# Loading and rotating the first batch under the table generation, and moving two weight casts from VectorE to ScalarE

## The chip, the cores and the metric

One core of a Trainium2 chip. The metric is the time of one execution on the device in microseconds (us), the median of several executions. "Span" is the profiler's length of one execution, from its first to its last instruction; it lies about 2 us under the time. The granted clock is the share of its full clock that TensorE gets; where it is 0.50 TensorE is called cold, at 1.00 warm. All runs told of here are in the fast state, with a mean granted clock of 0.97 to 1.00.

## The reference

A spectral mixing layer, then a two-layer network with an ELU between its layers, over 8 batches of 3008 x 256:

```python
X = np.fft.rfft(x, axis=1)                  # x: (8, 3008, 256) -> 1505 frequencies
Yr = Xr @ w_r - Xi @ w_i + b_r              # complex channel mixing, 256 x 256
Yi = Xr @ w_i + Xi @ w_r + b_i
Y  = soft_threshold(Yr, 0.01) + 1j * soft_threshold(Yi, 0.01)
y  = np.fft.irfft(Y, n=3008, axis=1)
h  = y.reshape(24064, 256) @ w_in           # 256 -> 2048
g  = np.where(h > 0, h, np.exp(np.minimum(h, 0)) - 1)
return g @ w_out                            # 2048 -> 256
```

## The kernel before

Both Fourier transforms are matmuls against tables of cosines and sines (`CT`, `ST`: 1505 x 1505, bf16), which the kernel generates itself, once, at its start. The real input is first folded: rows u(a) and v(S-a) give `ur` = u + v and `ui` = u - v ("the rotation": TensorE reverses the rows with a permutation matrix into `rps`, in PSUM, the memory space in which the kernel places the results of its matmuls; VectorE adds and subtracts). Then `fps` is the forward transform, `mps` the channel mixing, `psP`/`psQ` the inverse transform, `hps` and `ps_o` the network.

The set-up, with cuts marked:

```python
with tc.tile_pool(name="stagep", bufs=1) as stagep, tc.tile_pool(name="genp", bufs=2) as genp:
    # ... DMA of w_r, w_i, biases, then w_in_f and w_out_f (2 MB each), on SyncE's queue
    # ... four small casts of w_r, w_i to wcat_r, wcat_s
    nc.vector.tensor_scalar_mul(w_in_s_bf[:], w_in_f[:], s_scale)
    nc.vector.tensor_copy(w_out_r[:], w_out_f[:])
    # ... permutation matrices, index rows (brow, acol)
    for (g0, g1) in CH:                      # columns 0-512, 512-1024, 1024-1505
        for t in range(NT):                  # 12 tiles of 128 rows
            # ScalarE prod = brow*acol; VectorE qz (three operations); ScalarE ST = Sin(qz)
            # VectorE absw = |qz|;      ScalarE CT = Sin(pi/2 - absw)
    # ... two row scalings of CT by 0.5; column sum cs_ps of w_out_f and the bias rows bb_ps on TensorE

wk1 = ctx.enter_context(tc.tile_pool(name="wk1", bufs=1))
for b in range(B):
    Ut = wk1.tile([P, NT, D], F32R, name="Ut", tag="Ut")
    Vs = wk1.tile([P, NT, D], F32R, name="Vs", tag="Vs")
    # ... four nc.gpsimd.dma_start of batch b into Ut and Vs
    # ... rotation: rps -> ur, ui
    for kc, (k0, k1) in enumerate(CH):       # forward transform
        for comp, usrc, msrc, xdst in ((0, ur, CT, XrT), (1, ui, ST, XsT)):
            for dt in range(2):
                # 12 matmuls into fps, then nc.vector.tensor_copy(xdst[...], fps[...])
    # ... mps, psP, psQ, hps, ps_o, output
```

`wk1` is opened after the set-up pools are closed, so `Ut` and `Vs` lie where the set-up's tiles lay.

## Time and profile before

Median 1530.85 us (4 runs, 1530.05 to 1531.21), span 1528.7 us, mean granted clock 0.973. The prediction below reads the pieces of the set-up from the trace; they follow one another, weights, tables, load of batch 0, rotation and forward transform, and what comes behind them, 1389.3 us, is TensorE bound. The number to follow is the start of the first channel-mixing matmul (`mps`), called the milestone: 139.43. Columns of the order of time in the prediction: start us, us, engine, line, operation, out<-in, shapes, count, and in brackets the idle time before and what ended it.

```profile
3.96 0.42 DVE L93 TENSOR_SCALAR wcat_s<-w_r_f 128x512 bf16<-128x512 f32 x1
16.83 9.63 PE L166 MATMUL cs_ps<-w_out_f,ones_f 128*128 128x256 f32 x32 [16.83 <-DMA w_out_f<-in_moe_w_out_dram]
```

The small weight cast takes 0.42 us with nothing beside it, and the column sum runs at 16.83, under the tables, where it costs nothing.

### The profile page before, as it was taken

Reading aid. Unit: us, or ns where it says so; the run is one execution under the profiler, and the core shown is the slowest. Engines: PE = TensorE matmul, PEld = TensorE weight load, DVE = VectorE, ACT = ScalarE, POOL = GpSimd, SP = SyncE. Lnnn points to the kernel's source line nnn. Section 1 sums busy time; section 2 is a strip of 40 time slices with the busy share of each in tenths; the row PEclk is TensorE's granted clock in tenths of the full one; section 3 lists DMA queues with packets and bytes.
Section 4 is the critical chain, followed back from the end, with each engine's and each line's share of the span. In section 5 each row is a group of like instructions: output and inputs, shape, how many; then the busy total and the mean of one; then the engine's idle time right before and its main releaser. Section 6 shows DMA issues by size and latency. Waiting matters only on the chain.

```text
span 1528.7 us, 20423 instructions
## 1 busy us (share of the span) xinstructions
PE 1379.3 (90%) x7434; PEld 802.4 (52%) x7434; DVE 998.7 (65%) x1888; ACT 874.7 (57%) x1697; POOL 30.6 (2%) x45
## 2 busy tenths in 40 slices
PE   2039999989999899989999899999999899998998
PEld 2013466535664366635665356644665356643555
DVE  7945486565764587664875677654875657745666
ACT  6920199605992089703994069901996059920897
POOL 1010000000000000000000000000000000000000
PEclk8559999999999999999999999999999999999999
DMA  3061040000410040100400013000400000100001
GB/s 124 0 128 36 0 110 28 27 1 1 116 36 13 0 96 29 40 1 0 110 29 26 1 42 83 28 13 1 110 29 26 1 0 29 42 12 0 15 28 40
DMA packets 52905, 55.58 MB, mean 36 GB/s; under 512 B 1594, under 2 KB 52548, under 8 KB 52548
## 3 DMA queue, kind: packets, MB, share of 16 engines
q0 software_dynamic: 24960, 24.91, 7.6%
q1 hardware_dynamic: 27844, 29.37, 5.5%
q8 instruction: 58, 0.95, 0.3%
q14 instruction: 43, 0.35, 0.1%
HBM read 29.63 MB, written 24.64 MB: 36 GB/s over the span
## 4 chain that ended last, share of the span: by engine, by line
PE 80%; DVE 15%; issue 2%; DMA 1%; ACT 1%; POOL 0%; SPq 0%; DVEq 0%; ACTq 0%; POOLq 0%
PE ps_o L375 26%; PE fps L248 16%; PE hps L351 11%; PE hps L358 10%; PE psP L298 8%; PE psQ L310 8%; DVE yb L280 4%; DVE Yit L286 2%; DVE Yrt L283 2%; DVE gT L370 1%; DVE qz L148 1%; DVE absw L153 1%; DVE osb L385 1%; DVE qz L142 1%; DVE qz L145 1%
## 5 line engine op out<-in xcount | busy, mean ns | idle before, releaser
L370 DVE SCALAR_TENSOR_TENSOR gT<-Et,Rt 128x512 fp32r<-128x512 f32 (+1 forms) x768 | 518.6, 680 | 190.9 <-ACT Rt L369 140.1
L375 PE MATMUL ps_o<-w_out_r,gT 128*128 128x256 f32 (+1 forms) x3072 | 597.7, 317 | 7.9 <-DVE gT L370 6.2
L375 PEld LDWEIGHTS ps_o<-w_out_r,gT 128*128 128x128 f32 (+1 forms) x3072 | 428.8, 186 | 197.0 <-DVE gT L370 160.8
L366 ACT ACTIVATE Et<-hps 128x512 f32<-128x512 f32 (+1 forms) x768 | 455.2, 593 | 71.4 <-DVE gT L370 25.7
L369 ACT ACTIVATE Rt<-hps 128x512 bf16<-128x512 f32 (+1 forms) x768 | 452.5, 589 | 0.0
L306 ACT CAST Psb<-psP 128x512 bf16<-128x512 f32 (+1 forms) x48 | 27.8, 579 | 558.1 <-PE psP L298 558.1
L351 PE MATMUL hps<-yT,w_in_s_bf 128*128 128x512 bf16 (+1 forms) x768 | 294.8, 384 | 1.8 <-ACT Rt L369 1.7
L358 PE MATMUL hps<-yT,w_in_s_bf 128*128 128x512 bf16 (+1 forms) x768 | 288.3, 375 | 0.0
L248 PE MATMUL fps<-CTmat,ur 128*128 128x512 bf16 (+1 forms) x576 | 153.5, 379 | 0.5 <-DVE ui L232 0.5
L317 DVE TENSOR_TENSOR yT<-Psb,psQ 128x512 bf16<-128x512 bf16 (+1 forms) x48 | 32.6, 679 | 169.5 <-PE psQ L310 169.5
L248 PE MATMUL fps<-STmat,ui 128*128 128x512 bf16 (+1 forms) x576 | 140.3, 376 | 0.0
L298 PE MATMUL psP<-CTmat,Yrt 128*128 128x512 bf16 (+1 forms) x576 | 131.4, 375 | 4.7 <-DVE yb L280 4.7
L310 PE MATMUL psQ<-STmat,Yit 128*128 128x512 bf16 (+1 forms) x576 | 131.4, 375 | 0.0
L351 PEld LDWEIGHTS <-w_in_s_bf 128*128 128x128 bf16 x768 | 73.7, 96 | 44.5
L298 PEld LDWEIGHTS <-Yrt 128*128 128x128 bf16 x576 | 56.0, 97 | 74.3 <-issue 6.9
L310 PEld LDWEIGHTS <-Yit 128*128 128x128 bf16 x576 | 56.0, 97 | 65.4
L248 PEld LDWEIGHTS <-ur 128*128 128x128 bf16 x576 | 56.5, 98 | 64.1 <-issue 2.8
L248 PEld LDWEIGHTS <-ui 128*128 128x128 bf16 x576 | 53.9, 97 | 61.6 <-issue 1.0
L358 PEld LDWEIGHTS <-w_in_s_bf 128*128 128x128 bf16 x768 | 76.2, 99 | 14.2 <-issue 3.1
L255 DVE CAST XrT<-fps 128x512 bf16<-128x512 f32 (+1 forms) x48 | 32.7, 682 | 67.5 <-PE fps L248 67.5
L255 DVE CAST XsT<-fps 128x512 bf16<-128x512 f32 (+1 forms) x48 | 32.8, 683 | 66.0 <-PE fps L248 66.0
L385 DVE TENSOR_TENSOR osb<-ps_o,colsum_bc 128x256 f32<-128x256 f32 x192 | 67.8, 416 | 7.7 <-PE ps_o L375 7.0
(70 smaller groups left out, 759.0 us busy)
## 6 DMA issues: line engine op xcount, KB each, us to landing
out_dram<-osb SPq DMA_DIRECT2D x40, 512.0 KB, 2.8
Ut<-in_x_dram POOLq DMA_DIRECT2D x8, 1408.0 KB, 7.8
Vs<-in_x_dram POOLq DMA_DIRECT2D x8, 1408.0 KB, 9.3
out_dram<-osb SPq DMA_DIRECT2D x8, 384.0 KB, 2.5
w_in_f<-in_moe_w_in_dram SPq DMA_DIRECT2D x1, 2048.0 KB, 8.4
w_out_f<-in_moe_w_out_dram SPq DMA_DIRECT2D x1, 2048.0 KB, 13.8
Vs<-in_x_dram POOLq DMA_DIRECT2D x8, 128.0 KB, 2.9
Ut<-in_x_dram POOLq DMA_DIRECT2D x8, 97.0 KB, 6.9
```

Source lines behind the costliest of these rows:

```text
L248: nc.tensor.matmul(fps[:, 0:kw], lhsT=usrc[0:npt, t, dt * P : dt * P + P], rhs=msrc[0:npt, t, k0:k1], start=(t == 0), stop=(t == NT - 1),)
L255: nc.vector.tensor_copy(xdst[:, dt, k0:k1], fps[:, 0:kw])
L280: nc.vector.tensor_tensor(yb[0:kn], psk, bias_bc[0:kn, :], ALU.add)
L298: nc.tensor.matmul(psP[:, 0:nw], lhsT=Yrt[0:npt, t, dt * P : dt * P + P], rhs=CT[0:npt, t, n0:n1], start=(t == 0), stop=(t == NT - 1),)
L310: nc.tensor.matmul(psQ[:, 0:nw], lhsT=Yit[0:npt, t, dt * P : dt * P + P], rhs=ST[0:npt, t, n0:n1], start=(t == 0), stop=(t == NT - 1),)
L351: nc.tensor.matmul(hps[:, 0:nb], lhsT=w_in_s_bf[:, 0, ft * P : ft * P + P], rhs=yT[:, 0, bs:be], start=True, stop=False,)
L358: nc.tensor.matmul(hps[:, 0:nb], lhsT=w_in_s_bf[:, 1, ft * P : ft * P + P], rhs=yT[:, 1, bs:be], start=False, stop=True,)
L366: nc.scalar.activation(Et[:, 0:nb], hps[:, 0:nb], AF.Exp)
L369: nc.scalar.activation(Rt[:, 0:nb], hps[:, 0:nb], AF.Relu)
L370: nc.vector.scalar_tensor_tensor(gT[:, 0:nb], Et[:, 0:nb], 1.0, Rt[:, 0:nb], ALU.min, ALU.add)
L375: nc.tensor.matmul(ps_o[i][0:tn, :], lhsT=gT[:, t0:t1], rhs=w_out_r[:, ft, :], start=(ft == 0), stop=(ft == NFT - 1),)
L385: nc.vector.tensor_tensor(osb[0:tn, i, :], ps_o[i][0:tn, :], colsum_bc[0:tn, :], ALU.subtract)
```

## The change

Intent: give `Ut`, `Vs`, `ur` and `ui` memory of their own from the start, so that the first batch can be loaded and rotated while the tables are generated and its forward transform can follow them chunk by chunk; and take the two big weight casts out of VectorE's way. Core of the diff, cuts marked by `# ...`:

```diff
+    wk1a = ctx.enter_context(tc.tile_pool(name="wk1a", bufs=1))   # Ut, Vs, ur, ui, XrT, XsT
+    def emit_load(b):              # the four DMAs, body as before
+    def emit_rot(Ut, Vs):          # the rotation, body as before
+    def emit_main(b, ur, ui, pools):   # forward transform and all after it, as before
     with (stagep, genp):
-        w_r_f = stagep.tile([P, 2, D], F32, name="w_r_f")
+        w_st = wk1a.tile([P, NT // 2, D], F32, name="w_st", tag="ui")   # staging in ui's memory
         # ...
-        nc.vector.tensor_scalar_mul(w_in_s_bf[:], w_in_f[:], s_scale)
-        nc.vector.tensor_copy(w_out_r[:], w_out_f[:])
         # ... index rows now ahead of the permutation matrices
+        UV0 = emit_load(0)
         for (g0, g1) in CH:
             for t in range(NT):
                 # ... as before, but tabs[g0, t] = the absw operation, last_act = the cosine
-        nc.vector.tensor_scalar_mul(CT[0:1, 0, :], CT[0:1, 0, :], 0.5)      # and one more, over all columns
+            nc.vector.tensor_scalar_mul(CT[0:1, 0, g0:g1], ..., 0.5)        # and one more, per chunk
+            if g0 == 0:
+                with tc.issue_after(tabs[0, 10].ins):
+                    ur0, ui0 = emit_rot(*UV0)
+        with tc.issue_after(last_act.ins):
+            nc.scalar.activation(w_in_s_bf[:], w_in_f[:], AF.Copy, bias=0.0, scale=s_scale)
+            nc.scalar.copy(w_out_r[:], w_out_f[:])
         # ... column sum and bias rows as before
+    # ... wk1b (Yrt, Yit, yT), wk2, wk3
+    for b in range(B):
+        if b == 0:
+            ur, ui = ur0, ui0
+        else:
+            ur, ui = emit_rot(*emit_load(b))
+        emit_main(b, ur, ui, pools)
```

`issue_after` places what stands under it behind the named instruction in its engine's order.

More of the change, by code (lines that the diff above doesn't have):

```diff
@@ L71 @@
     psO = ctx.enter_context(tc.tile_pool(name="psO", bufs=4, space=bass.MemoryType.PSUM))
-    with (
-        tc.tile_pool(name="stagep", bufs=1) as stagep,
-        tc.tile_pool(name="genp", bufs=2) as genp,
-    ):
-        w_r_f = stagep.tile([P, 2, D], F32, name="w_r_f")
-        nc.sync.dma_start(w_r_f[:], w_r.rearrange("(c p) e -> p c e", p=P))
-        w_i_f = stagep.tile([P, 2, D], F32, name="w_i_f")
-        nc.sync.dma_start(w_i_f[:], w_i.rearrange("(c p) e -> p c e", p=P))
-        b_r_row = stagep.tile([1, D], F32, name="b_r_row")
-        b_i_row = stagep.tile([1, D], F32, name="b_i_row")
-        nc.sync.dma_start(b_r_row[:], b_r.rearrange("(o d) -> o d", o=1))
-        nc.sync.dma_start(b_i_row[:], b_i.rearrange("(o d) -> o d", o=1))
-        w_in_f = stagep.tile([P, 2, DFF], F32, name="w_in_f")
-        nc.sync.dma_start(w_in_f[:], moe_w_in.rearrange("(c p) f -> p c f", p=P))
-        w_out_f = stagep.tile([P, NFT, E], F32, name="w_out_f")
-        nc.sync.dma_start(w_out_f[:], moe_w_out.rearrange("(t p) e -> p t e", p=P))
-        nc.vector.tensor_copy(wcat_r[:, :, 0:D], w_r_f[:])
-        nc.vector.tensor_copy(wcat_r[:, :, D : 2 * D], w_i_f[:])
-        nc.vector.tensor_copy(wcat_s[:, :, 0:D], w_i_f[:])
-        nc.vector.tensor_scalar_mul(wcat_s[:, :, D : 2 * D], w_r_f[:], -1.0)
-        nc.vector.tensor_scalar_mul(w_in_s_bf[:], w_in_f[:], s_scale)
-        nc.vector.tensor_copy(w_out_r[:], w_out_f[:])
-        nc.gpsimd.memset(ones_f[:], 1.0)
-        jtmp = genp.tile([P, P], F32, name="jtmp", tag="jt")
-        nc.gpsimd.memset(jtmp[:], 0.0)
-        nc.gpsimd.affine_select(
-            out=jtmp[:], in_=jtmp[:], pattern=[[1, P]], compare_op=ALU.not_equal,
-            fill=1.0, base=-(P - 1), channel_multiplier=1,
-        )
-        nc.vector.tensor_copy(J_mid[:], jtmp[:])
-        jtmp2 = genp.tile([P, P], F32, name="jtmp2", tag="jt")
-        nc.gpsimd.memset(jtmp2[:], 0.0)
-        nc.gpsimd.affine_select(
-            out=jtmp2[:], in_=jtmp2[:], pattern=[[1, P]], compare_op=ALU.not_equal,
-            fill=1.0, base=-P, channel_multiplier=1,
-        )
-        nc.vector.tensor_copy(J_first[:], jtmp2[:])
-        jtmp3 = genp.tile([P, P], F32, name="jtmp3", tag="jt")
-        nc.gpsimd.memset(jtmp3[:], 0.0)
-        nc.gpsimd.affine_select(
-            out=jtmp3[:], in_=jtmp3[:], pattern=[[1, P]], compare_op=ALU.not_equal,
-            fill=1.0, base=0, channel_multiplier=1,
-        )
-        nc.vector.tensor_copy(E00[:], jtmp3[:])
-        brow_i = genp.tile([P, F], I32, name="brow_i", tag="gi")
-        nc.gpsimd.iota(brow_i[:], pattern=[[1, F]], base=0, channel_multiplier=0)
-        acol_i = genp.tile([P, NT], I32, name="acol_i", tag="gi2")
-        nc.gpsimd.iota(acol_i[:], pattern=[[P, NT]], base=0, channel_multiplier=1)
-        brow = genp.tile([P, F], F32, name="brow", tag="g0")
-        nc.vector.tensor_copy(brow[:], brow_i[:])
-        acol = genp.tile([P, NT], F32, name="acol", tag="g3")
-        nc.vector.tensor_copy(acol[:], acol_i[:])
-        sin_scale = 2.0 * math.pi / S * (1.0 - 3e-7)
-        invS = 1.0 / S
-        CMAGIC = 12582912.0
-        cbias = genp.tile([P, 1], F32, name="cbias", tag="cb")
-        nc.vector.memset(cbias[:], math.pi / 2.0)
-        for (g0, g1) in CH:
-            gw = g1 - g0
-            for t in range(NT):
-                prod = genp.tile([P, 512], F32, name="prod", tag="g1")
-                nc.scalar.activation(
-                    prod[:, 0:gw], brow[:, g0:g1], AF.Copy, bias=0.0, scale=acol[:, t : t + 1]
-                )
-                qz = genp.tile([P, 512], F32, name="qz", tag="g2")
-                nc.vector.tensor_scalar(
-                    qz[:, 0:gw], prod[:, 0:gw], invS, CMAGIC, ALU.mult, ALU.add
-                )
-                nc.vector.tensor_scalar(
-                    qz[:, 0:gw], qz[:, 0:gw], -CMAGIC, -float(S), ALU.add, ALU.mult
-                )
-                nc.vector.tensor_tensor(qz[:, 0:gw], qz[:, 0:gw], prod[:, 0:gw], ALU.add)
-                nc.scalar.activation(
-                    ST[:, t, g0:g1], qz[:, 0:gw], AF.Sin, bias=0.0, scale=sin_scale
-                )
-                absw = genp.tile([P, 512], F32, name="absw", tag="g3b")
-                nc.vector.scalar_tensor_tensor(
-                    absw[:, 0:gw], qz[:, 0:gw], -1.0, qz[:, 0:gw], ALU.mult, ALU.max
-                )
-                nc.scalar.activation(
-                    CT[:, t, g0:g1], absw[:, 0:gw], AF.Sin, bias=cbias[:], scale=-sin_scale
-                )
-        nc.vector.tensor_scalar_mul(CT[0:1, 0, :], CT[0:1, 0, :], 0.5)
-        nc.vector.tensor_scalar_mul(
-            CT[LASTP - 1 : LASTP, NT - 1, :], CT[LASTP - 1 : LASTP, NT - 1, :], 0.5
-        )
-        cs_ps = psAcc.tile([P, 512], F32, name="cs_ps", tag="acc")
-        for ft in range(NFT):
-            nc.tensor.matmul(
-                cs_ps[:, 0:E],
-                lhsT=ones_f[:, 0:P],
-                rhs=w_out_f[:, ft, :],
-                start=(ft == 0),
-                stop=(ft == NFT - 1),
-            )
-        nc.scalar.copy(colsum_bc[:], cs_ps[:, 0:E])
-        bcatF = stagep.tile([1, 2 * D], F32, name="bcatF")
-        nc.vector.tensor_copy(bcatF[:, 0:D], b_r_row[:])
-        nc.vector.tensor_copy(bcatF[:, D : 2 * D], b_i_row[:])
-        bb_ps = psAcc.tile([P, 512], F32, name="bb_ps", tag="acc")
-        nc.tensor.matmul(bb_ps[:, 0 : 2 * D], lhsT=ones_f[0:1, 0:P], rhs=bcatF[:, :], start=True, stop=True)
-        nc.scalar.copy(bias_bc[:], bb_ps[:, 0 : 2 * D])
@@ L182 @@
-    wk1 = ctx.enter_context(tc.tile_pool(name="wk1", bufs=1))
-    wk2 = ctx.enter_context(tc.tile_pool(name="wk2", bufs=2))
-    wk3 = ctx.enter_context(tc.tile_pool(name="wk3", bufs=3))
+    wk1a = ctx.enter_context(tc.tile_pool(name="wk1a", bufs=1))
     out2d = out
-    for b in range(B):
+    def emit_load(b):
         xb = x[b]
-        Ut = wk1.tile([P, NT, D], F32R, name="Ut", tag="Ut")
-        Vs = wk1.tile([P, NT, D], F32R, name="Vs", tag="Vs")
+        Ut = wk1a.tile([P, NT, D], F32R, name="Ut", tag="Ut")
+        Vs = wk1a.tile([P, NT, D], F32R, name="Vs", tag="Vs")
@@ L204 @@
         )
-        ur = wk1.tile([P, NT, D], BF16, name="ur", tag="ur")
-        ui = wk1.tile([P, NT, D], BF16, name="ui", tag="ui")
+        return Ut, Vs
+    def emit_rot(Ut, Vs):
+        ur = wk1a.tile([P, NT, D], BF16, name="ur", tag="ur")
+        ui = wk1a.tile([P, NT, D], BF16, name="ui", tag="ui")
         for j in range(NT // 2):
@@ L234 @@
                 )
-        XrT = wk1.tile([P, 2, F], BF16, name="XrT", tag="XrT")
-        XsT = wk1.tile([P, 2, F], BF16, name="XsT", tag="XsT")
+        return ur, ui
+    def emit_main(b, ur, ui, pools):
+        wk1b, wk2, wk3 = pools
+        XrT = wk1a.tile([P, 2, F], BF16, name="XrT", tag="XrT")
+        XsT = wk1a.tile([P, 2, F], BF16, name="XsT", tag="XsT")
         for kc, (k0, k1) in enumerate(CH):
@@ L255 @@
                     nc.vector.tensor_copy(xdst[:, dt, k0:k1], fps[:, 0:kw])
-        Yrt = wk1.tile([P, NT, D], BF16, name="Yrt", tag="Yrt")
-        Yit = wk1.tile([P, NT, D], BF16, name="Yit", tag="Yit")
+        Yrt = wk1b.tile([P, NT, D], BF16, name="Yrt", tag="Yrt")
+        Yit = wk1b.tile([P, NT, D], BF16, name="Yit", tag="Yit")
         for kt in range(NT):
@@ L289 @@
             )
-        yT = wk1.tile([P, 2, S], BF16, name="yT", tag="yT")
+        yT = wk1b.tile([P, 2, S], BF16, name="yT", tag="yT")
         for dt in range(2):
@@ L399 @@
                 )
+    with (
+        tc.tile_pool(name="stagep", bufs=1) as stagep,
+        tc.tile_pool(name="genp", bufs=2) as genp,
+    ):
+        w_st = wk1a.tile([P, NT // 2, D], F32, name="w_st", tag="ui")
+        w_r_f = w_st[:, 0:2, :]
+        nc.sync.dma_start(w_r_f, w_r.rearrange("(c p) e -> p c e", p=P))
+        w_i_f = w_st[:, 2:4, :]
+        nc.sync.dma_start(w_i_f, w_i.rearrange("(c p) e -> p c e", p=P))
+        b_r_row = stagep.tile([1, D], F32, name="b_r_row")
+        b_i_row = stagep.tile([1, D], F32, name="b_i_row")
+        nc.sync.dma_start(b_r_row[:], b_r.rearrange("(o d) -> o d", o=1))
+        nc.sync.dma_start(b_i_row[:], b_i.rearrange("(o d) -> o d", o=1))
+        w_in_f = stagep.tile([P, 2, DFF], F32, name="w_in_f")
+        nc.sync.dma_start(w_in_f[:], moe_w_in.rearrange("(c p) f -> p c f", p=P))
+        w_out_f = stagep.tile([P, NFT, E], F32, name="w_out_f")
+        nc.sync.dma_start(w_out_f[:], moe_w_out.rearrange("(t p) e -> p t e", p=P))
+        nc.vector.tensor_copy(wcat_r[:, :, 0:D], w_r_f)
+        nc.vector.tensor_copy(wcat_r[:, :, D : 2 * D], w_i_f)
+        nc.vector.tensor_copy(wcat_s[:, :, 0:D], w_i_f)
+        nc.vector.tensor_scalar_mul(wcat_s[:, :, D : 2 * D], w_r_f, -1.0)
+        brow_i = wk1a.tile([P, NT * D // 2], I32, name="brow_i", tag="ur")
+        nc.gpsimd.iota(brow_i[:, 0:F], pattern=[[1, F]], base=0, channel_multiplier=0)
+        acol_i = stagep.tile([P, NT], I32, name="acol_i")
+        nc.gpsimd.iota(acol_i[:], pattern=[[P, NT]], base=0, channel_multiplier=1)
+        brow = stagep.tile([P, F], F32, name="brow")
+        nc.vector.tensor_copy(brow[:], brow_i[:, 0:F])
+        acol = stagep.tile([P, NT], F32, name="acol")
+        nc.vector.tensor_copy(acol[:], acol_i[:])
+        nc.gpsimd.memset(ones_f[:], 1.0)
+        jtmp = stagep.tile([P, P], F32, name="jtmp")
+        nc.gpsimd.memset(jtmp[:], 0.0)
+        nc.gpsimd.affine_select(
+            out=jtmp[:], in_=jtmp[:], pattern=[[1, P]], compare_op=ALU.not_equal,
+            fill=1.0, base=-(P - 1), channel_multiplier=1,
+        )
+        nc.vector.tensor_copy(J_mid[:], jtmp[:])
+        jtmp2 = stagep.tile([P, P], F32, name="jtmp2")
+        nc.gpsimd.memset(jtmp2[:], 0.0)
+        nc.gpsimd.affine_select(
+            out=jtmp2[:], in_=jtmp2[:], pattern=[[1, P]], compare_op=ALU.not_equal,
+            fill=1.0, base=-P, channel_multiplier=1,
+        )
+        nc.vector.tensor_copy(J_first[:], jtmp2[:])
+        jtmp3 = stagep.tile([P, P], F32, name="jtmp3")
+        nc.gpsimd.memset(jtmp3[:], 0.0)
+        nc.gpsimd.affine_select(
+            out=jtmp3[:], in_=jtmp3[:], pattern=[[1, P]], compare_op=ALU.not_equal,
+            fill=1.0, base=0, channel_multiplier=1,
+        )
+        nc.vector.tensor_copy(E00[:], jtmp3[:])
+        UV0 = emit_load(0)
+        tabs = {}
+        sin_scale = 2.0 * math.pi / S * (1.0 - 3e-7)
+        invS = 1.0 / S
+        CMAGIC = 12582912.0
+        cbias = stagep.tile([P, 1], F32, name="cbias")
+        nc.vector.memset(cbias[:], math.pi / 2.0)
+        for (g0, g1) in CH:
+            gw = g1 - g0
+            for t in range(NT):
+                prod = genp.tile([P, 512], F32, name="prod", tag="g1")
+                nc.scalar.activation(
+                    prod[:, 0:gw], brow[:, g0:g1], AF.Copy, bias=0.0, scale=acol[:, t : t + 1]
+                )
+                qz = genp.tile([P, 512], F32, name="qz", tag="g2")
+                nc.vector.tensor_scalar(
+                    qz[:, 0:gw], prod[:, 0:gw], invS, CMAGIC, ALU.mult, ALU.add
+                )
+                nc.vector.tensor_scalar(
+                    qz[:, 0:gw], qz[:, 0:gw], -CMAGIC, -float(S), ALU.add, ALU.mult
+                )
+                nc.vector.tensor_tensor(qz[:, 0:gw], qz[:, 0:gw], prod[:, 0:gw], ALU.add)
+                nc.scalar.activation(
+                    ST[:, t, g0:g1], qz[:, 0:gw], AF.Sin, bias=0.0, scale=sin_scale
+                )
+                absw = genp.tile([P, 512], F32, name="absw", tag="g3b")
+                tabs[g0, t] = nc.vector.scalar_tensor_tensor(
+                    absw[:, 0:gw], qz[:, 0:gw], -1.0, qz[:, 0:gw], ALU.mult, ALU.max
+                )
+                last_act = nc.scalar.activation(
+                    CT[:, t, g0:g1], absw[:, 0:gw], AF.Sin, bias=cbias[:], scale=-sin_scale
+                )
+            nc.vector.tensor_scalar_mul(CT[0:1, 0, g0:g1], CT[0:1, 0, g0:g1], 0.5)
+            nc.vector.tensor_scalar_mul(
+                CT[LASTP - 1 : LASTP, NT - 1, g0:g1], CT[LASTP - 1 : LASTP, NT - 1, g0:g1], 0.5
+            )
+            if g0 == 0:
[4 more added lines that the diff above has]
+            nc.scalar.copy(w_out_r[:], w_out_f[:])
+        cs_ps = psAcc.tile([P, 512], F32, name="cs_ps", tag="acc")
+        for ft in range(NFT):
+            nc.tensor.matmul(
+                cs_ps[:, 0:E],
+                lhsT=ones_f[:, 0:P],
+                rhs=w_out_f[:, ft, :],
+                start=(ft == 0),
+                stop=(ft == NFT - 1),
+            )
+        nc.scalar.copy(colsum_bc[:], cs_ps[:, 0:E])
+        bcatF = stagep.tile([1, 2 * D], F32, name="bcatF")
+        nc.vector.tensor_copy(bcatF[:, 0:D], b_r_row[:])
+        nc.vector.tensor_copy(bcatF[:, D : 2 * D], b_i_row[:])
+        bb_ps = psAcc.tile([P, 512], F32, name="bb_ps", tag="acc")
+        nc.tensor.matmul(
+            bb_ps[:, 0 : 2 * D], lhsT=ones_f[0:1, 0:P], rhs=bcatF[:, :],
+            start=True, stop=True,
+        )
+        nc.scalar.copy(bias_bc[:], bb_ps[:, 0 : 2 * D])
@@ L403 @@
+    wk1b = ctx.enter_context(tc.tile_pool(name="wk1b", bufs=1))
+    wk2 = ctx.enter_context(tc.tile_pool(name="wk2", bufs=2))
+    wk3 = ctx.enter_context(tc.tile_pool(name="wk3", bufs=3))
+    pools = (wk1b, wk2, wk3)
+    for b in range(B):
[4 more added lines that the diff above has]
+        emit_main(b, ur, ui, pools)
 _INS = ['x', 'w_r', 'w_i', 'b_r', 'b_i', 'moe_w_in', 'moe_w_out']
```

## The prediction

> **What bounds the kernel now.** I read the slices first, then busy time by stretch, then the long waits, then the order of time around the set-up.
>
> The slices of the page (40 of 38.2 us each):
>
> ```profile
> PE   2039999989999899989999899999999899998998
> DVE  7945486565764587664875677654875657745666
> ...
> PEclk8559999999999999999999999999999999999999
> ```
>
> TensorE is 90% busy or more from the fourth slice to the end. Only the first three slices, some 115 us, have it idle, and its granted clock falls to 0.5 there. So the kernel is TensorE bound except for a set-up at the front. Busy time by stretch (columns: stretch, length, then busy time and instruction count of PE, PEld, DVE, ACT, POOL, then clock, DMA share, GB/s):
>
> ```profile
> 0.00:13.00 13.00, 0.00 (x0) 0.00 (x0) 5.50 (x13) 3.90 (x4) 4.01 (x13) 1.00 0.84 294
> 31.00:62.00 31.00, 0.00 (x0) 0.00 (x0) 30.59 (x64) 28.50 (x48) 0.00 (x0) 0.50 0.00 1
> 86.40:107.15 20.75, 4.96 (x14) 3.37 (x15) 7.31 (x22) 0.00 (x0) 3.66 (x5) 0.50 0.78 150
> 107.15:139.20 32.05, 32.05 (x143) 14.30 (x143) 8.81 (x15) 0.00 (x0) 3.04 (x4) 0.95 0.48 98
> ```
>
> In the second line VectorE works 30.59 of 31 us: it generates the cosine and sine tables (CT, ST) and bounds that stage, with ScalarE close behind (28.50). Third: the loads and the rotation of batch 0 with DVE two thirds idle and DMA busy. Fourth: the forward transform of batch 0 (fps), pure TensorE. From the list of waits in the first 110 us (what waited, for what: us, times, longest), and from the order of time:
>
> ```profile
> POOL Ut L192 <- ACT CTmat L156: 79.9, 1, 79.9
> PE rps L214 <- issue: 68.4, 1, 68.4
> ```
>
> ```profile
> 10.83 2.29 DVE L94 TENSOR_SCALAR w_in_s_bf<-w_in_f 128x4096 bf16<-128x4096 f32 x1 [3.39 <-DMA w_in_f<-in_moe_w_in_dram]
> 13.04 0.76 DVE L142 TENSOR_SCALAR qz<-prod 128x512 f32<-128x512 f32 x2
> 17.59 2.29 DVE L95 CAST w_out_r<-w_out_f 128x4096 fp32r<-128x4096 f32 x1
> 86.39 0.55 DVE L160 TENSOR_SCALAR CTmat<-CTmat 1x1505 bf16<-1x1505 bf16 x1 [0.76 <-ACT CTmat L156]
> 86.98 1.22 POOL L192 DMA_DIRECT2D Ut<-in_x_dram  x1 [79.87 <-ACT CTmat L156]
> 99.76 1.01 PE L221 MATMUL rps<-Vs,J_mid 128*128 128x256 f32 x3 [3.08 <-DMA Vs<-in_x_dram]
> 107.15 7.05 PE L248 MATMUL fps<-CTmat,ur 128*128 128x512 bf16 x24 [0.53 <-DVE ui L232]
> 139.43 0.38 PE L263 MATMUL mps<-wcat_r,XrT 128*128 128x512 bf16 x1
> ```
>
> The load of batch 0 does not start before the last table write: its tiles lie in memory that the set-up pool frees only then. So the pieces stand in a row: 13.0 us before the first table step, 73.9 us of tables (with one 2.2 us cast in them), 12.8 us of load (86.98 to 99.76), 7.4 us of rotation, 32.3 us of transform. The channel mixing (mps) starts at 139.43; I take that as the milestone.
>
> [...] the clock was 0.50 until 110 us and 1.00 from 111.5, and fps matmuls started every 0.43 us at first, then every 0.216. [...]
>
> **The change, part by part.** The order of the built programs shows that from the first inverse transform (psP) on, every engine executes the same sequence in both kernels. So all gain or loss is the shift of the milestone, unless a transfer time changes.
>
> 1. The big weight casts leave VectorE: 2.29 us (w_in_s_bf, with 3.39 us of waiting for its DMA) and 2.2 us (w_out_r). They go to ScalarE after its last table step. First table step: VectorE does its four weight casts from 3.62, two bias copies, brow (0.93), acol, and ScalarE's first product takes 0.71; I get 7.3 instead of 13.04.
>
> 2. The load is issued from about 3.6 us, beside w_in_f and w_out_f. Bytes in flight: 2+2+0.5+3 MB = 7.5 MB; before, 4.5 MB had landed by 16.8, some 310 GB/s from 2.4 us. So 7.5 MB lands near 26 us. The rotation needs it at about 29.5.
>
> 3. Table chunk 0 (12 steps): a step of 512 columns took 1.98 us, of 481 columns 1.90 (24 x 1.98 + 12 x 1.90 = 70.4; measured from 13.04 to 85.62, less 2.2, also 70.4). 7.3 + 12 x 1.98 + 0.3 for small operations = 31.4.
>
> 4. The rotation sits in VectorE's order right behind chunk 0: 24 operations at 0.333 us from start to start = 8.0, plus 0.15: 39.5.
>
> 5. In TensorE's order the column sum (cs_ps, 9.63 us before) stands behind the rotation. It can start when the fifth rps buffer is read, 38.2, and ends at 47.8, the bias matmul at 48.9. ScalarE holds its copies after table step 3 of chunk 1, so it stands from about 46.5 to 49.6; VectorE runs out of products after five steps (49.1) and waits until 50.9: a stall of about 1.8 us. The first fps groups run from 48.9.
>
> 6. Chunk 1: 12 x 1.98 + 0.4 for the row scalings + 1.8 stall + four fps casts. A cast takes 0.69, some 0.6 from start to start, and fills a gap of 0.1 that dependent steps leave, so 0.5 each: 2.0. 39.5 + 23.8 + 0.4 + 1.8 + 2.0 = 67.5.
>
> 7. Chunk 2: 12 x 1.90 + 0.2 + 2.0 = 25.0: 92.5. The last cosine on ScalarE and the row scaling: 93.5.
>
> 8. TensorE takes fps chunks 0 and 1 under the tables, and of chunk 2 the 22 cosine matmuls whose table rows exist. Left after 93.5: two cosine matmuls, a cast that frees a PSUM buffer (together about 1.4), then 24 sine matmuls. Warm 24 x 0.204 = 4.9; [...] I take 6.3. Mixing starts at 93.5 + 1.4 + 6.3 = 101.2.
>
> Shift: 139.4 - 101.2 = 38.2 us. 1530.85 - 38.2 = 1492.6 us.
>
> As a cross-check: removed are 5.7 us at the start, 2.2 us of cast, 12.8 us of load, and 24.4 of the 32.05 us of transform (7.7 stay), 45.1 in all; paid back are 4 us of casts and 1.8 us of stall, with 1 us of small operations and hand-overs. That leaves 38.3.
>
> **The rivals.** A: *the load is late.* [...] Margin is about 3.5 us; if it lands at 35, VectorE, in order, stands for 5 us: 1498. [...] For it: nothing here has shown this overlap.
>
> B: *the moved casts become the bound.* The first bias add (yb) now also waits for the w_out_r copy on ScalarE: their buffers share memory. [...] yb is due at 101.2 + 1.06 = 102.3. [...]
>
> C: *VectorE becomes worse than a sum.* Casts wait in its order for TensorE groups and stop table steps behind them. If each of the eight costs 1.2 instead of 0.5 us, and the column-sum stall is 4 us: +8 us, 1500. Against: in the order most casts stand several steps after their group should end.
>
> D: *more is hidden.* If the trickle of matmuls keeps the array warm and the stall vanishes: 3.5 us better, 1489.
>
> E: *the shift is given back later.* Against: same order from psP on, and PE is 90% busy from slice four; there is no slack in which a head start would drown.
>
> **Range and chances.** Most of the removed row is certain (the load and most of the transform do come out of it). A, B and C are each some 15 to 20% likely and cost about 5 to 8 us; D gives 4. So 1488 to 1500 for 8 in 10. The 2% line is 1500.2, a milestone later than 108.8; it takes two rivals at once, or one much worse than drawn. Faster 0.89, same 0.1, slower 0.01. Central 1493.
>
> **What would show it.** First table step at 7.3; load landed by 26; rotation over at 39.5; last table at 93.5; mixing at 101. Right: TensorE works in slices two and three, and the wait of GpSimd for the last cosine is gone. Wrong: a long VectorE wait on Ut or Vs (A), yb waiting on ScalarE (B), gaps before the fps casts (C), or a distance from mixing to end unlike 1528.7 - 139.4 = 1389.3 us (E).

## The result, and the profile after

The changed kernel takes 1493.83 us (median of 8 runs, 1492.13 to 1494.24), against 1531.44 for the kernel before in the same rounds (12 runs). The ratio is 0.9753, 95% interval 0.9743 to 0.9763: faster by 2.5%. (Ratios here are the mean time of one kernel's fast runs over that of the other's fast runs of the same rounds, so not quite the ratio of the medians.) Span 1491.9, clock 0.994. Later, beside other kernels, it ran again: 1493.60, ratio 0.9756 [0.9743, 0.9769].

The 40 slices of the page after, 37.3 us each:

```profile
PE   1779999899998999989998999989999899999998
...
PEclk9989999999999999999999999999999999999999
```

TensorE now works seven tenths of the second and third slices. From the fourth on it is as busy as before. In PEclk the two slices at 0.5 are gone; but the clock records of this trace begin at 44.68 us, so the 9 of the first slice says nothing, and TensorE was cold again from 72.0 to 78.8 and from 92.5 to 99.3. The same stretches of time as in the prediction's table:

```profile
31.00:62.00 31.00, 24.03 (x87) 14.65 (x88) 29.14 (x68) 18.67 (x33) 3.37 (x4) 1.00 0.50 101
86.40:107.15 20.75, 15.73 (x59) 6.25 (x59) 13.16 (x28) 13.06 (x12) 0.00 (x0) 0.84 0.00 0
```

In the first, VectorE is as busy as before (29.14 of 31 us; 30.59 before), but TensorE now works 24.03 us where it had worked none. The second held the load and the rotation; now it holds the end of the transform and the start of the mixing. From the order of time of the changed kernel:

```profile
3.33 1.35 POOL L81 DMA_DIRECT2D Ut<-in_x_dram  x1
3.94 0.96 DVE L317 TENSOR_SCALAR wcat_s<-w_st 128x512 bf16<-128x512 f32 x1
7.80 0.57 DVE L367 TENSOR_SCALAR qz<-prod 128x512 f32<-128x512 f32 x1 [0.55 <-ACT prod L363]
25.86 1.01 PE L113 MATMUL rps<-Vs,J_mid 128*128 128x256 f32 x3 [4.63 <-DMA Vs<-in_x_dram]
38.89 10.00 PE L398 MATMUL cs_ps<-w_out_f,ones_f 128*128 128x256 f32 x32 [0.58 <-issue]
51.73 0.43 DVE L367 TENSOR_SCALAR qz<-prod 128x512 f32<-128x512 f32 x1 [1.70 <-ACT prod L363]
94.03 0.28 DVE L385 TENSOR_SCALAR CTmat<-CTmat 1x481 bf16<-1x481 bf16 x1 [0.76 <-ACT CTmat L381]
95.68 6.82 PE L143 MATMUL fps<-STmat,ui 128*128 128x481 bf16 x24 [0.35 <-DVE XrT L150]
97.41 3.59 ACT L394 CAST w_out_r<-w_out_f 128x4096 fp32r<-128x4096 f32 x1
102.34 0.38 PE L158 MATMUL mps<-wcat_r,XrT 128*128 128x512 bf16 x1
103.46 0.69 DVE L175 TENSOR_TENSOR yb<-mps,bias_bc 128x512 f32<-128x512 f32 x1 [0.26 <-PE mps L170]
```

The load is issued at 3.33 and has landed at 25.86. The column sum, 10.00 us, now stands between the rotation and the transform in TensorE's order. ScalarE's copies behind it hold the products back, and VectorE stands 1.70 us at 51.73 for want of one. The tables end at 94.03, the milestone is at 102.34, and 1491.9 - 102.34 = 1389.6 us follow it, where 1389.3 followed before. So the whole change of time is the shift of the milestone: 139.43 - 102.34 = 37.1 us in the profiled executions, 37.6 in the medians. In the list of waits of the first 140 us, GpSimd's wait of 79.9 us for the last cosine is gone, and what GpSimd waits for instead is the next batch's turn:

```profile
POOL Vs L89 <- PE rps L113: 30.5, 1, 30.5
```

### The profile page after: what moved, and what is told of

It reads as the page before. It is cut to its first block, busy times and chain, and to the rows that moved or that the text cites.

```text
span 1491.9 us, 20427 instructions
## 1 busy us (share of the span) xinstructions
PE 1383.8 (93%) x7434; PEld 802.8 (54%) x7434; DVE 994.2 (67%) x1890; ACT 882.3 (59%) x1699; POOL 30.5 (2%) x45
## 4 chain that ended last, share of the span: by engine, by line
PE 81%; DVE 15%; issue 2%; ACT 1%; DMA 0%; DVEq 0%; ACTq 0%
PE ps_o L270 27%; PE fps L143 15%; PE hps L246 11%; PE hps L253 10%; PE psP L193 8%; PE psQ L205 8%; DVE yb L175 4%; DVE Yit L181 2%; DVE Yrt L178 2%; DVE gT L265 2%; DVE absw L378 1%; DVE qz L373 1%; DVE osb L280 1%; DVE qz L367 1%; PE cs_ps L398 1%
## 5 line engine op out<-in xcount | busy, mean ns | idle before, releaser
L143 PE MATMUL fps<-CTmat,ur 128*128 128x512 bf16 (+2 forms) x576 | 153.6, 377 | 9.1 <-DVE CTmat L385 3.8
L143 PE MATMUL fps<-STmat,ui 128*128 128x512 bf16 (+1 forms) x576 | 143.8, 383 | 6.9 <-DVE XrT L150 6.9
L143 PEld LDWEIGHTS <-ur 128*128 128x128 bf16 (+1 forms) x576 | 55.9, 97 | 73.7 <-issue 10.7
L253 PEld LDWEIGHTS <-w_in_s_bf 128*128 128x128 bf16 x768 | 76.2, 99 | 14.1 <-issue 3.2
L158 PE MATMUL mps<-wcat_r,XrT 128*128 128x512 bf16 x96 | 36.2, 377 | 37.5 <-DVE yb L175 37.2
## 6 DMA issues: line engine op xcount, KB each, us to landing
w_out_f<-in_moe_w_out_dram SPq DMA_DIRECT2D x1, 2048.0 KB, 20.3
```

The lines of the kernel that those rows point to most:

```text
L143: nc.tensor.matmul(fps[:, 0:kw], lhsT=usrc[0:npt, t, dt * P : dt * P + P], rhs=msrc[0:npt, t, k0:k1], start=(t == 0), stop=(t == NT - 1),)
L158: nc.tensor.matmul(psk, lhsT=XrT[:, 0, kt * P : kt * P + kn], rhs=wcat_r[:, 0, :], start=True, stop=False,)
L253: nc.tensor.matmul(hps[:, 0:nb], lhsT=w_in_s_bf[:, 1, ft * P : ft * P + P], rhs=yT[:, 1, bs:be], start=False, stop=True,)
```

## The experiments

Nine runs, all correct. "Milestone" is that of the profiled execution.

| run | what it is | median us | ratio to before [95%] | milestone | span less milestone |
|---|---|---|---|---|---|
| e1_load_late | casts and start changed, load and rotation after the tables | 1524.83 | 0.9960 [0.9945, 0.9975] | 133.22 | 1389.7 |
| e2_rot_late | load early, rotation after the tables | 1511.43 | 0.9874 [0.9857, 0.9890] | 119.13 | 1389.9 |
| e3_casts_dve | the change, big casts left on VectorE | 1506.19 | 0.9838 [0.9823, 0.9853] | 114.74 | 1389.6 |
| e4_dup_casts | the change, eight `fps` casts done twice | 1495.95 | 0.9772 [0.9757, 0.9786] | 104.33 | 1389.8 |
| e5_warm | the change, 18 unread matmuls | 1491.31 | 0.9745 [0.9730, 0.9759] | 99.92 | 1389.4 |
| e6_cs_late | the change, column sum before the rotation | 1491.88 | 0.9750 [0.9736, 0.9765] | 100.77 | 1390.2 |
| e7_mirror | the change, half of each table row by reversed copies | 1470.61 | 0.9609 [0.9593, 0.9625] | 80.04 | 1389.5 |
| e8_warm_cs | e5 and e6 together | 1493.02 | 0.9752 [0.9738, 0.9765] | 100.29 | 1389.6 |
| e9_after_again | the change itself | 1493.60 | 0.9756 [0.9743, 0.9769] | 100.88 | 1389.7 |

The last column is the first finding: over nine variants what follows the milestone keeps its length within 0.9 us. Whatever a variant wins at the milestone it keeps.

### e1_load_late: no early load, no early rotation

```diff
-        UV0 = emit_load(0)                      # before the tables
         # ... tables, without emit_rot behind chunk 0
+        UV0 = emit_load(0, CT[:, NT - 1, F - 1 : F])   # its tiles first written from the last table column
+        with tc.issue_after(last_dve.ins):
+            ur0, ui0 = emit_rot(*UV0)
```

(`cs_ps` and `bb_ps` get buffers of another pool, and their ScalarE copies stand after the tables.)

> The changed kernel, with the load of batch 0 held back until the last table entry is written, and the rotation and the forward transform of batch 0 behind it (column sum in other PSUM buffers, so that it waits for nothing). What stays of the change: the weight casts on ScalarE and the earlier first table step. Theory (the milestone, the first mixing matmul, moves by what leaves the row in front): tables end near 80, load lands near 93.4, rotation 7.4, transform 32.3: mixing near 133, time near 1524, so that the casts and the start alone are worth about 7 us. Rival (the later stages run better with the new buffers, whatever happens in front): time well under 1520 while mixing starts near 133.

Measured: 1524.83 us, milestone 133.22. From its order of time:

```profile
79.95 1.23 POOL L86 DMA_DIRECT2D Ut<-in_x_dram  x1
```

The load is issued at 79.95 (86.98 before), and the old row follows it: load, rotation, transform. The casts and the reordered start together are worth 139.43 - 133.22 = 6.2 us at the milestone (7.0 at the issue of the load; the load, and the first 24 `fps` matmuls, 7.46 us for 7.05, took a little longer here).

### e2_rot_late: early load, no early rotation

```diff
-            if g0 == 0:
-                with tc.issue_after(tabs[0, 10].ins):
-                    ur0, ui0 = emit_rot(*UV0)
+        with tc.issue_after(last_dve.ins):      # behind the last row scaling
+            ur0, ui0 = emit_rot(*UV0)
```

(Column sum, bias row and ScalarE's copies as in e1.)

> As the changed kernel, load at the front, but rotation and forward transform of batch 0 behind all tables. Theory: tables end near 80.4, rotation and transform in a row, mixing near 119.5, time near 1511; so the early load alone is worth 13 us against the run before and the overlap of rotation and transform with the tables 17 us net of what it costs VectorE. Rival (the load is the gain, the overlap is given back as VectorE is the bound there and has to do rotation and evictions anyway): time within 3 us of the changed kernel, 1494 to 1497.

Measured: 1511.43 us, milestone 119.13. The early load alone is worth 133.22 - 119.13 = 14.1 us, a little more than the 12.8 us for which the rotation had waited on it. From here to the change as given, 119.13 - 102.34 = 16.8 us come from the rotation and transform that lie under the tables, less the stall behind the column sum, which e1 and e2 do not have. The three parts sum to the 37.1 us of the milestone by construction (each is a difference of neighbours); what they tell is the sizes: 6.2, 14.1, 16.8.

### e3_casts_dve: the big casts back on VectorE

```diff
+        nc.vector.tensor_scalar_mul(w_in_s_bf[:], w_in_f[:], s_scale)
+        nc.vector.tensor_copy(w_out_r[:], w_out_f[:])
         # ... tables
-        with tc.issue_after(last_act.ins):
-            nc.scalar.activation(w_in_s_bf[:], w_in_f[:], AF.Copy, bias=0.0, scale=s_scale)
-            nc.scalar.copy(w_out_r[:], w_out_f[:])
```

> The changed kernel with the two big weight casts back on VectorE, where they stood. Theory: VectorE stands in its order at w_in_f (lands near 11.1) and again at w_out_f, which lands at 23.2 in the changed kernel because the early load shares the transfers; so the first table step comes at 13.4 and the third or so at 25.5, some 14 us later than in the changed kernel: time near 1507. Rival (only the 4.5 us of cast work count, waits are hidden): time near 1498.

Measured: 1506.19 us, milestone 114.74, which is 12.4 us later than with the change (some 14 expected): as the theory of waits had it, not the rival that counted the cast work alone (4.5 us, the 2.29 and 2.2 of the prediction). From the list of waits of this run (engine, what waited, for what: us, times, longest):

```profile
DVE w_out_r L319 <- DMA w_out_f<-in_moe_w_out_dram: 5.6, 1, 5.6
DVE w_in_s_bf L318 <- DMA w_in_f<-in_moe_w_in_dram: 4.2, 1, 4.2
```

In VectorE's order the casts stand ahead of the table steps, so the tables waited these 4.2 and 5.6 us for 4 MB of weights, which are in flight together with the early load: `w_out_f` took 13.8 us from issue to landing before, and 20.3 in the changed kernel, with the early load beside it. The early load therefore needs the casts moved: kept where they were, they would give back a third of the gain.

### e4_dup_casts: what one fps cast costs

```diff
                     nc.vector.tensor_copy(xdst[:, dt, k0:k1], fps[:, 0:kw])
+                    if b == 0 and kc < 2:
+                        nc.vector.tensor_copy(xdst[:, dt, k0:k1], fps[:, 0:kw])
```

> The changed kernel with each of the eight evictions of fps that lie among the table steps done twice. Theory: VectorE bounds the table stage and an eviction costs it 0.5 to 0.6 us there, so the milestone moves by 4 to 5 us: time 1498 to 1499. Rival (the stage is paced by the ping-pong between VectorE and ScalarE, evictions fill gaps): under 2 us, below 1496. The first evictions of a pair also come one step earlier or later in the order than in the changed kernel, which may add a wait for TensorE.

Measured: 1495.95 us, only 2.1 us above the change (2.9 by the ratios): under the 1498 to 1499 of the theory, and at the edge of what its rival forecast (under 2 us, below 1496). The first step of the expectation held. The last `absw`, first line from the change and the others from e4, moves by 3.79 us, or 0.47 for each of the eight casts (VectorE's stall for a product was 1.33 us in e4, not 1.70; with these 0.37 us it is 0.52). So the rival's mechanism, casts that fill gaps, is out:

```profile
92.60 0.66 DVE L378 SCALAR_TENSOR_TENSOR absw<-qz 128x481 f32<-128x481 f32 x1
```

```profile
96.39 0.66 DVE L380 SCALAR_TENSOR_TENSOR absw<-qz 128x481 f32<-128x481 f32 x1
99.44 5.06 PE L143 MATMUL fps<-STmat,ui 128*128 128x481 bf16 x24 [0.55 <-DVE XrT L150]
```

What failed is what comes after: the last 24 sine matmuls took 4.9 us from the first to the milestone at 104.33, where the change took 6.66 (95.68 to 102.34). The later tables had piled up cosine matmuls right before them (15 in a row from 93.87), and TensorE was at full rate when they began, at 99.44: the granted clock was 0.50 from 96 to 98 us, 0.87 from 98 to 100 and 1.00 from 100 to 104, where 12 started in every 2 us. That gave the next experiment its question.

### e5_warm: keep TensorE busy through the end of the tables

```diff
+                        nd = {8: 5, 9: 7, 10: 3}.get(t, 0)
+                        if b == 0 and kc == 2 and comp == 0 and dt == 1 and nd:
+                            with tc.issue_after(mm.ins):
+                                for _ in range(nd):     # results are never read
+                                    nc.tensor.matmul(dump[:, :], lhsT=CT[:, 0, 0:P], rhs=CT[:, 0, 0:512],
+                                                     start=True, stop=True)
```

> The changed kernel with 18 matmuls that nobody reads, put between the last cosine matmuls of batch 0's third chunk, where TensorE otherwise trickles; VectorE's and ScalarE's orders are the same as in the changed kernel. Theory (the last 24 sine matmuls took 6.7 us there because the clock fell to 0.50 during the trickle; run e4 took 4.9 at 1.00): the clock stays at 1.00, the last group takes 4.9, mixing starts near 100.6 instead of 102.3 and the time is 1.5 to 1.8 us shorter than the changed kernel's, near 1492.1. Rival (the group was slow for another reason, as the PSUM slot or the ScalarE copies of the weights): no gain, or the first bias add waits for ScalarE instead.

Measured: 1491.31 us (1490.57 to 1491.53), milestone 99.92, both a little under the theory's. Busy time by stretch, first of the change, then of e5 (columns: stretch, length; PE, PEld, DVE, ACT and POOL busy with counts; granted clock, DMA share, GB/s):

```profile
92.00:94.00 2.00, 0.80 (x2) 0.23 (x2) 1.16 (x2) 1.52 (x4) 0.00 (x0) 0.62 0.00 0
96.00:98.00 2.00, 2.00 (x6) 0.75 (x5) 0.19 (x1) 2.00 (x2) 0.00 (x0) 0.50 0.00 0
```

```profile
92.00:94.00 2.00, 1.77 (x9) 0.78 (x8) 0.98 (x3) 1.77 (x3) 0.00 (x0) 1.00 0.00 0
96.00:98.00 2.00, 2.00 (x11) 0.97 (x10) 0.33 (x1) 2.00 (x2) 0.00 (x0) 1.00 0.00 0
```

With the change, TensorE is busy 40% of the stretch from 92 to 94 and its clock falls (0.62 there, 0.50 from 94 to 98); the sine matmuls then start cold, 6 in 2 us. With the unread matmuls the clock stays at 1.00 and 11 start in 2 us; the sine group takes 4.9 us again. That the clock made e4 cheap, and costs the change some 1.8 us (6.66 - 4.9) in its first profile, 1.1 in its second (5.99), is thereby shown. The whole shift, 2.4 us, holds another 0.5 us from elsewhere: VectorE's stall for a product was 1.04 in this execution, not 1.70 (more of that under e9). As a gain over the change e5 is small: all four of its executions lie below all thirteen of the change (1492.13 to 1494.24), but they were taken in different calls, in which the kernel before was 1.3 us apart (1530.11 and 1531.44). The ratios, 0.9745 and 0.9753, leave some 1.2 us, and their intervals overlap.

### e6_cs_late: take the stall away

```diff
+        X0 = new_x()
+        emit_fwd(ur0, ui0, *X0, (0,))       # chunk 0 of the transform first
         # ... cs_ps (in another pool's buffer) and bb_ps
+        emit_fwd(ur0, ui0, *X0, (1, 2))
         # ... all ScalarE copies behind last_act
```

> The changed kernel with the column sum and the bias row in PSUM buffers of the later stage, their copies on ScalarE behind the last table step; TensorE computes them before the rotation. Theory: the 1.7 us that VectorE stood for a product behind those copies goes, but TensorE is in the column sum until about 34.6 and the third pair of the rotation waits about 0.7 for it: mixing near 101.2, time about 1 us shorter than the changed kernel's, near 1492.8. Rival (that stall hid other waits): no change, within 0.4 us; or the column sum delays the rotation by more, up to 4 us longer.

In the source the column sum stands behind chunk 0, but in the program that was built it comes before the rotation, as the expectation has it: in the trace it starts at 23.26 and ends at 32.4.

Measured: 1491.88 us, milestone 100.77. The stall is gone (VectorE's waits for a product sum to 0.6 us in the whole set-up), and the tables end about 2 us earlier than in the first profile of the change, near 92.3 (1.2 earlier than in its second). But the milestone moved by 1.6 only, since the last group ran slowly:

```profile
93.65 7.28 PE L146 MATMUL fps<-STmat,ui 128*128 128x481 bf16 x24 [0.35 <-DVE XrT L153]
```

From there to 100.77 are 7.1 us, against 6.66 in the first profile of the change and 4.9 in e5 with the clock at 1.00: slow matmuls take back part of what an earlier end of the tables buys. As a gain in time it is not shown: the ratios, 0.9750 and 0.9753, differ by 0.5 us, and the second profile of the change has its milestone at 100.88.

### e8_warm_cs: both at once

Edit: e6, with e5's unread matmuls behind the same three matmuls. (What the expectation calls the late column sum is e6's; it runs before the rotation here too, from 23.4 us.)

> The late column sum (which took the 1.7 us stall away and ended the tables some 2 us earlier) together with the 18 unread matmuls that kept the granted clock at 1.00. Theory that the clock ate part of the late column sum's gain: the sine group now starts near 93.6 us as with the late column sum alone, takes 4.9 instead of 7.1, and the mixing starts at 98.4 to 98.8, so the time is 1489.5 to 1490.2. Rival that the two act on the same thing and do not add: mixing no earlier than with the warm clock alone, 99.9, 1491.3. If the unread matmuls, which stand in TensorE's order before the last cosine matmuls, push the last cosine matmuls back instead: 1491 to 1493.

Measured: 1493.02 us (4 runs, 1491.78 to 1493.86), no better than either alone, and its interval covers that of the change: the third of the three expectations, 1491 to 1493, fits best. From its order of time:

```profile
91.94 3.40 PE L157 MATMUL dump<-CTmat 128*128 128x512 bf16 x15
95.39 5.06 PE L146 MATMUL fps<-STmat,ui 128*128 128x481 bf16 x24
```

The clock held (1.00 in every stretch from 90 to 104 us, 4.9 us for the sine group), but in the order that was built 15 of the 18 unread matmuls stood in one row before the last cosine matmul, 3.2 us long, and pushed the sine group to 95.39. So this run does not tell whether the two gains add; it shows that work put in to keep the clock up costs time where it stands in front of work that is ready.

### e9_after_again: how far two executions of the same kernel differ

> The changed kernel again, on the same chip and in the same rounds, so that the 1 to 4 us between it and the variant can be read with an interval. Expected 1493.8, mixing at 102.3.

Measured: 1493.60 us, as expected; but its profiled execution, 1492.54, had the milestone at 100.88, 1.5 us before that of the first profile. In order of time:

```profile
38.89 8.94 PE L398 MATMUL cs_ps<-w_out_f,ones_f 128*128 128x256 f32 x32 [0.57 <-issue]
50.67 0.43 DVE L367 TENSOR_SCALAR qz<-prod 128x512 f32<-128x512 f32 x1 [0.64 <-ACT prod L363]
```

The same column sum, started at the same 38.89, took 8.94 us, not 10.00, and so VectorE's stall was 0.64, not 1.70. By stretch (first of the first profile, then of this one):

```profile
42.00:44.00 2.00, 2.00 (x6) 1.61 (x5) 2.00 (x5) 1.33 (x3) 0.15 (x1) 1.00 1.39 357
```

```profile
42.00:44.00 2.00, 2.00 (x10) 1.73 (x9) 2.00 (x5) 1.33 (x3) 0.15 (x1) 1.00 1.38 355
```

Until 42 both start some three matmuls per us; in this execution five per us from 42 on, in the other only later. (The transfers beside them are alike, 357 and 355 GB/s.) The clock column reads 1.00 in all these stretches, but that is where the views have no record. The clock records in the trace files begin, with a change to 1.00, at 44.68 us in the first profile, 42.53 in this one, 43.34 in e5 and 43.92 in e4. The column sum started at 38.88 or 38.89 in all four; in e5 it took 9.34 us, and in e4

```profile
38.88 9.63 PE L400 MATMUL cs_ps<-w_out_f,ones_f 128*128 128x256 f32 x32 [0.57 <-issue]
```

So in the order of the release, 42.53, 43.34, 43.92 and 44.68, the sum takes 8.94, 9.34, 9.63 and 10.00 us, and VectorE's stall is 0.64, 1.04, 1.33 and 1.70: every microsecond of half clock more costs half a microsecond. The starts of its matmuls agree: from 42 to 44 us 10, 8, 6 and 6 in the same order, from 44 to 46 us 11, 11, 11 and 9. So the moment of warming up differed by up to 2.15 us between executions, and it is this that changed the column sum. The set-up's length differs by 1.5 us between two executions of one kernel, and single profiles of e5, e6 and e8 are to be read with that in mind.

### e7_mirror: generate half the table and copy the other half

(The column sum runs before the rotation, as in e6, and eight table steps are placed behind `fps` casts in VectorE's order; the diff leaves the latter out.) The table's row a at column 1504 - k is its value at k up to a sign that depends on the row alone: cos(pi a - x) = (-1)^a cos x, and sin(pi a - x) = -(-1)^a sin x. So only columns 0 to 752 are generated, and the rest are reversed copies times a sign per partition:

```diff
-        for (g0, g1) in CH:
+        for (g0, g1) in ((0, 512), (512, H // 2 + 1)):       # H = 1504
             for t in range(NT):
                 # ... prod, qz, ST, absw, CT as before
+                nc.vector.tensor_scalar_mul(ST[:, t, r0 : r1 : -1], ST[:, t, g0:m1], sgn[:, 5:6])
+                # ... row scaling of CT where t is the first or last
+                nc.vector.tensor_scalar_mul(CT[:, t, r0 : r1 : -1], CT[:, t, g0:m1], sgn[:, 4:5])
             if g0 == 0:
                 # ... rotation as before
+                casts = emit_fwd(ur0, ui0, *X0, (0, 2))      # chunks 0 and 2, while the middle is generated
+        # ... column sum, then emit_fwd(ur0, ui0, *X0, (1,))
```

> A further step than the change: half of the tables (columns 0 to 752) is generated, the other half is copied from it in reverse order with the sign of the row's parity (two VectorE copies per step in place of a step), with the column sum as in e6 and fps chunks in the order 0, 2, 1, their evictions pinned in VectorE's order. Theory (VectorE's table work sets the milestone until TensorE's 31 us of fps behind the rotation does): with copies of 0.3 to 0.6 us for 512 elements the tables end at 72 to 81, mixing starts at 80 to 89, time 1472 to 1481. The weight casts on ScalarE then end about when the first bias add is due, and may take over as the wait there. Rival (the front is bound by something else than the table steps: the load or ScalarE): time above 1488.

Measured: 1470.61 us (4 runs, 1469.97 to 1471.30), ratio 0.9609 [0.9593, 0.9625]: 22 to 23 us below the change (by the ratios, by the medians) and 4% below the kernel before, and correct. Time and milestone (80.04) lie at or just under the lower ends of what was expected. From its order of time:

```profile
14.06 0.34 DVE L426 TENSOR_SCALAR CTmat<-CTmat,sgn 128x512 bf16<-128x512 bf16 x1
14.32 0.34 DVE L417 TENSOR_SCALAR STmat<-STmat,sgn 128x512 bf16<-128x512 bf16 x1
45.75 8.09 PE L147 MATMUL fps<-CTmat,ur 128*128 128x512 bf16 x24 [0.53 <-DVE ui L124]
53.68 5.36 PE L147 MATMUL fps<-STmat,ui 128*128 128x512 bf16 x24
```

and by stretch:

```profile
50.00:70.00 20.00, 20.00 (x94) 9.14 (x93) 18.51 (x63) 10.77 (x26) 0.00 (x0) 0.97 0.64 127
```

A reversed copy of 512 columns costs 0.26 us from start to start, so some 0.5 us for both tables, where generating 512 columns of both took a step of 1.98. Now TensorE works 20.00 of 20 us from 50 to 70: from the end of the rotation, at 45.75, the bound has gone from VectorE to TensorE. The first 24 `fps` matmuls take 8.09 us, cold for the greater part (granted clock 0.50 from 40 to 50 us, 0.97 over 50 to 70); the remaining 120 need 26 more. So the stage was still bound by the generation of the tables after the change: with half of it the milestone moved by 22.3 us (the column sum before the rotation, which this kernel has too, moved it by 1.6 in e6; the order of the chunks and the placing of the steps were not run alone).

## Why the prediction was right

It said 1493.0 (1488 to 1500, 0.89 for faster by over 2%), and 1493.8 came. By its own steps:

- *Step 1, start of the tables.* Predicted 7.3, measured 7.80. This is its largest miss in one place. In the trace one of the small weight casts took 0.96 us where it took 0.42 before, and the first `qz` 0.57 where others take 0.43, each beside a DMA issue of GpSimd (the first of them runs from 3.33 to 4.68, over the small cast's start at 3.94); in e1, without that load, the small cast took 0.42 and the first step began at 7.23. GpSimd's four issues were longer too, in sum (1.35, 0.78, 1.29 and 1.08 us, and 1.22, 0.58, 0.59 and 1.08 in the kernel before). The 7.3 had allowed nothing for this; why the two are slower beside one another was not shown.
- *Step 2, landing.* Predicted 26, needed 29.5; the last wait for it ended at 25.86, and the rotation's first add came at 30.46. Rival A (the load is late) did not occur.
- *Steps 3 and 4.* Rotation over at 40.03, predicted 39.5: the half microsecond of step 1 carried through.
- *Step 5.* Column sum 38.2 to 47.8, measured 38.89 to 48.89; stall 1.8, measured 1.70 in the first profile and 0.64 in the second. The mechanism was right; that 1.8 lies so near to 1.70 is luck, since the size follows the moment at which the clock is released (e9), which the prediction did not consider.
- *Steps 6 and 7.* Last scaling done 93.5, measured 94.03 to 94.31. From the end of the rotation to there 54.0 us were predicted and 54.3 measured. The casts' 0.5 us each is 0.47 to 0.52 by e4. Rival C (casts worse than their sum) did not occur.
- *Step 8.* Milestone 101.2, measured 102.34 and 100.88. The sine group was taken as 6.3, the estimate, for 4.9 warm; it took 6.66 and 5.99. That the clock falls there (0.50 from 94 to 98 us), and costs 1.1 to 1.8 us, was rightly in rival D, and e5 shows it.
- *Rival B.* That ScalarE's big copies would be done before the first `yb` was the estimate; no trace before had shown copies of this size on ScalarE. They took 3.60 and 3.59 us and end at 101.0, and the first `yb`, at 103.46, waits for its matmul alone.
- *Rival E.* 1389.3 us after the milestone before, 1389.6 after, and 1389.4 to 1390.2 in all variants: nothing is given back. (That TensorE is 90% busy from the fourth slice on was read a little too high: seven of those slices show an 8. Nothing hung on it.)

The cross-check sum of the prediction had 45.1 us removed and 6.8 paid back. The experiments divide the gain otherwise, by part of the change, and there one thing had not been said: the casts, with the reordered start, are worth 6.2 us without the early load (e1), but the casts by themselves 12.4 under it (e3), because the early load delays the very weights that they wait for. The parts of this change do not stand beside one another; two of them need each other.

The time was hit within 0.8 us, less than the 1.5 us by which two executions' milestones differ; so near a hit is partly luck. What stays open: whether the warm clock and the moved column sum add (e8 did not test it).

## What to carry to other kernels

Before a set-up is rearranged, pick one milestone behind which the order of every engine is unchanged: a gain there is kept in full, and every variant can be judged by it. When a load is moved ahead, look for what else waits on transfers in flight beside it (here `w_out_f`, 20.3 us to landing for 13.8), and take those waits out of the order of the engine that bounds the stage. And once work is hidden under a stage, ask what the stage itself costs: halving the table generation brought 22 us more at the milestone, while rearranging what lies under it brought at most 2.4, in single profiles that differ by 1.5 from one execution to the next.

## What the traces show of the clock and of the DMA issues

- The granted clock fell at 92.47 us in the change's first profile, though the longest idle gap of TensorE from 86 us on was 1.67 us. TensorE was busy 0.57 of the 2 us from 90 to 92 and 0.80 of those from 92 to 94. With 1.46 and 1.77 us of the same stretches busy (e5) the clock stayed at 1.00. How busy TensorE must be for that was not shown.
- The views do not say what holds before the first clock record: it lies at 21.87 us in the trace before and at 44.68 in the first of the change, the clock column prints 1.00 until then, and TensorE worked slower all the same (6 starts of the column sum from 42 to 44 us in the first profile, 11 from 46 to 48). From the first record on, the records fit the rates (e9).
- Beside the DMA issues of one batch on GpSimd, a 128x512 operation of VectorE took 0.96 us for 0.42, and the tables started 0.57 us later than without them (7.80 against 7.23 in e1).
